# y's transposes queued behind the convolution's copies, loads a step further ahead of the sums

## The chip, the cores and the metric

The kernel runs on one core of a Trainium2 chip. The metric is the device time of one launch in microseconds. The version before took 1355.53 us (median of three runs, 1351.73 to 1358.41). Its profile was taken on one further execution of 1354.19 us, whose trace spans 1352.3 us.

## The reference, cut to what matters

```python
# x: (8, 4160, 192) f32, weight: (8, 7); w_in: (192, 1024) f64, w_out: (1024, 192) f64, g_ln: (1024,)
w = softmax(weight, axis=-1)                       # per head: 7 taps
x_pad = concatenate([zeros((B, 6, D)), x], axis=1) # causal, each of 8 batches by itself
y = einsum('hk,bskhg->bshg', w, windows of x_pad)  # 8 heads of 24 columns
h = y.reshape(33280, 192) @ w_in
e = exp(h - max(h)); solu = h * e / (sum(e) + 1e-9)
ln = (solu - mean(solu)) / sqrt(var(solu) + 1e-6) * g_ln
out = ln @ w_out                                   # (33280, 192) f32
```

## The kernel before

**Tiles, steps, chunks.** The 33280 rows are 260 tiles of 128 rows. From tile 8 on the loop takes three tiles a step (`three_steps`, tiles i, i+1, i+2, called a, b and c; i = 8, 11, 14, ...). x comes in 17 chunks: chunks 0 to 2 have 8, 8 and 16 tiles, chunks 3 to 14 have 16, the last two 18. Since 16 is no multiple of three, the steps cut the chunks in three ways that take turns. In chunks 3, 6, 9 and 12 tiles 12, 13, 14 are a step and tile 15 stands in the next one, ahead of tiles 0 and 1 of the chunk that follows (kind A). In chunks 2, 5, 8 and 11 tiles 13, 14, 15 are a step (kind B). In chunks 4, 7, 10 and 13 tiles 11, 12, 13 are one and 14, 15, 0 the next (kind C).

**What a tile passes through.** TensorE multiplies the transposed y (`yT`) with w_in in two f16 parts, `whi` and `wlo`, into `ph` (L813, L836; the smaller third part also reads `y2`). VectorE takes the row maximum (L867, `emit_max`), ScalarE the exponential (L874), VectorE the product (L884), ScalarE the f16 upper part `p` (L892) and the squares (L896), GpSimd the f16 rest (L904). SyncE then issues the DMA that transposes p into `pT` (L906). Three to five tiles later TensorE multiplies pT with w_out into `po` (L936), VectorE empties that bank (L946), GpSimd scales the rows (L1015), SyncE stores two tiles at a time (L1028).

**What a chunk passes through, ahead of its tiles.** Chunks from 3 on are `Strips`. Four loads (L354, 48 partitions and 576 KB each; numbers 0 to 3) bring x into one of two buffer sets, named `xs` and `xr` in the profile, which the chunks take in turn. Loads 0 and 1 fill the two partition halves of the first tile of the set, loads 2 and 3 those of the second. Four sums on VectorE (L375, `peak` in the table) take the absolute maximum; the sums 0 and 1 each read all partitions of the first tile, so both need loads 0 and 1, and the sums 2 and 3 need loads 2 and 3. The maxima set the scale `s`. Four convolutions on TensorE (L398, into two PSUM banks `pc`), each followed by ScalarE's copy (L278, `upper`) and VectorE's (L287, `lower`), write `y16`. SyncE's DMA transposes (L427, `turn`) carry y16 into `yT` in six pieces: two halves of block 1, and two each of blocks 0 and 2; block 1 is complete after the second convolution, blocks 0 and 2 after the fourth. One plain DMA (L435, `double`) copies a part into `y2`. In seven chunks load 0 holds the start of a batch: GpSimd then clears 16 rows of it (L363), which waits for that load's landing, and GpSimd's later work stands behind.

**What sets the order.** Every engine works through its own instructions in the order in which the code emits them; all DMAs of the main loop stand in SyncE's (SP's). `chores` (from L1071) is a table: for tile k of chunk ch it lists what is done for chunks ch+1 (convolutions, open, turns), ch+2 (loads, peaks) and ch+3 (loads). A step collects the entries of its three tiles. Loads are emitted at the step's start, ahead of its stores and of its p's transposes; peaks and `lower` ahead of `emit_max(a)`. Turns collected in a step are put in the list `moves` at its end; `move()` takes one from the list at three places: behind a's p, behind b's, and at the end. The banks `pc` and `po` are two that take turns, so a product into `po` waits for VectorE's copy out of the bank.

**The beginning.** `first_two` to `fourth_two` handle tiles 0 to 7. The unused rows between the halves of the strips are cleared once by DMAs (L451, `clear`): both tiles of `xs` and three loads of chunk 3 stand ahead of tile 6's p. Chunk 4's four loads are all emitted in the step of tiles 20 to 22, the first sum of it in the same step.

Of the kernel before, what the change touches and what calls it, by code (L numbers as in the profile page):

```python
# [19 lines left out]
def kernel(  # L20
# [309 lines left out]
    class Strips(Chunk):  # L330


        def __init__(self, ch):
            self.ch = ch
            self.b, self.t0, self.n = spans[ch]
            self.nt = self.n // P
            self.np = 4
# [10 lines left out]
        def load(self, j):  # L348

            half, late, t = self.place(j)  # L350
            self.raw[j] = t
            nt, own = self.nt, slice(64 * half, 64 * half + ROWS)
            first = self.t0 + late * nt * P // 2 + Q * ((half + late) % 2) - HALO
            nc.sync.dma_start(  # L354
                t[own],
                bass.AP(
                    tensor=x.tensor, offset=first * D,
                    ap=[[D, ROWS], [2 * Q * D, nt], [1, D]],
                ),
            )  # L360
            for w in range(nt):
                if (first + HALO + 2 * Q * w) % S == 0:
                    pool.memset(t[64 * half : 64 * half + HALO, w, :], 0.0)  # L363
# [19 lines left out]
        def product(self, h, n, a, z, bank=None):  # L383

            m = self.nt // 2
            banks = [single(f"pc_{self.ch}_{h}_{late}") for late in range(2)]
# [27 lines left out]
        def lower(self, pc, h, n, a, b):  # L414
            m = self.nt // 2
            for late in range(2):
                super().lower(pc[late], h, n, late * m, (late + 1) * m)
# [644 lines left out]
    def chores(ch, k, n):  # L1062
# [29 lines left out]
        else:  # L1092
# [179 lines left out]
    def third_two(i):  # L1272
# [31 lines left out]
        clear(0, 1)  # L1304
# [8 lines left out]
    def fourth_two(i):  # L1313
# [28 lines left out]
        early.clear()  # L1342
        emit_square(t)
# [21 lines left out]
    def three_steps(i):  # L1365
# [4 lines left out]
        work = others(ts)  # L1370
        todo = [lambda q=q: (q[0], *conv(*q)) for q in work.get("conv", [])]
# [40 lines left out]
        def lowers(n):  # L1412
            for k, pc, hg in at(n):
                k.lower(pc, *hg)
# [27 lines left out]
        if soon:  # L1442
            turns()
# [89 lines left out]
        if start:  # L1533
            for k, h in work.get("peak", []):
                sum_up(k, h, i + 2)
# [16 lines left out]
        else:  # L1552
            opens()
            if not soon:
                turns()
# [98 lines left out]
```

## Time and profile before

| | |
|---|---|
| time, median of three runs | 1355.53 us |
| the profiled execution | 1354.19 us, span 1352.3 us |
| busy: TensorE / VectorE / ScalarE / GpSimd | 1160.2 / 998.4 / 961.4 / 756.3 us |
| VectorE, sums (L375) of xr and xs | 49.6 and 49.5 us, 28 each |
| p's transposes (pT<-p, SP) | 263, median 4.7 us from issue to landing |
| y's transposes (yT<-y, SP) | 102, median 3.7 us |
| moved by DMA | 234.15 MB on one hardware queue |

A row of a timeline gives the start, the length, the engine, the line, the operation and the tiles written and read, and in brackets the engine's idle time before it and what ended that. A q behind an engine's name marks its sequencer: an SP row's length is the time in which SP waits for what the DMA needs and hands it over, not the transfer's. A row of waits names who waited, for whom, the sum in us, how often, and the longest.

### The profile page before, as it was taken

To read this page: it belongs to the slowest core of one execution; us is meant where nothing else is said; L and a number is where in the kernel's file an instruction comes from. 1 tells how busy PE (TensorE), PEld (TensorE's weight loads), DVE (VectorE), ACT (ScalarE), POOL (GpSimd) and SP (SyncE) were. 2 spreads that over 40 slices of the span, in tenths; PEclk is the share of its full clock that TensorE was granted. 3 is DMA by queue.
4 is the path that set the end of the run, shared out by engine and by line. 5 is a ranking of instruction groups with operands and counts; after the bars stand their busy time and mean duration, and the time that the engine had idled before them with its cause. 6 is when DMAs were issued, how large, how long until landed. Compare 5 with 4: busy or idle time off the path is not lost.

```text
span 1352.3 us, 24085 instructions
## 1 busy us (share of the span) xinstructions
PE 1160.2 (86%) x8854; PEld 667.0 (49%) x8854; DVE 998.4 (74%) x1736; ACT 961.4 (71%) x1613; POOL 756.3 (56%) x748
## 2 busy tenths in 40 slices
PE   5958486997989979699897979889796997999998
PEld 3635243553545545355454545445453554555556
DVE  8846285885858768586886868678685886887777
ACT  7936365784867858578685768668585785888886
POOL 3445254473664746547546655656464664666774
PEclk9979888998989989899998989899897998999999
DMA  8799889999989999999999999999999999999978
GB/s 221 129 139 170 149 143 168 174 162 180 172 151 199 177 177 180 173 169 179 192 188 170 180 185 178 156 185 191 175 175 178 174 180 167 184 195 175 197 159 174
DMA packets 736180, 235.68 MB, mean 174 GB/s; under 512 B 649230, under 2 KB 734654, under 8 KB 736062
## 3 DMA queue, kind: packets, MB, share of 16 engines
q1 hardware_dynamic: 736062, 234.15, 100.2%
q8 instruction: 69, 1.13, 0.3%
q14 instruction: 49, 0.40, 0.1%
HBM read 40.50 MB, written 25.56 MB: 49 GB/s over the span
## 4 chain that ended last, share of the span: by engine, by line
PE 26%; POOL 19%; issue 17%; DMA 16%; DVE 10%; ACT 7%; SPq 6%; POOLq 0%; DVEq 0%; ACTq 0%
POOL p L904 13%; PE po L936 12%; PE ph L813 11%; DMA xr<-in_x_dram 5%; DMA xs<-in_x_dram 5%; SPq L906 4%; DVE e L884 3%; DVE ph L867 2%; POOL raw L1015 2%; ACT e L874 2%; DMA pT<-p 2%; POOL t L1007 2%; ACT p L892 2%; DMA yT<-y 2%; ACT sq L896 2%
## 5 line engine op out<-in xcount | busy, mean ns | idle before, releaser
L904 POOL TENSOR_TENSOR p<-e,p 128x1024 f16<-128x1024 f32 x257 | 546.8, 2136 | 441.3 <-ACT p L892 416.2
L936 PE MATMUL po<-ohl,pT 128*128 128x192 f16 (+1 forms) x4264 | 565.3, 291 | 92.2 <-DVE y L287 68.7
L936 PEld LDWEIGHTS <-pT 128*128 128x128 f16 x4264 | 396.3, 100 | 268.2 <-issue 98.2
L813 PE MATMUL ph<-whi,yT 128*128 128x512 f16 x1548 | 428.4, 386 | 69.4 <-DMA yT<-y 66.7
L874 ACT ACTIVATE e<-ph,sm 128x1024 f32<-128x1024 f32 x260 | 289.6, 1114 | 259.3 <-DVE ph L867 237.2
L884 DVE SCALAR_TENSOR_TENSOR e<-ph,cv,e 128x1024 f32<-128x1024 f32 x259 | 331.6, 1280 | 73.5 <-ACT e L874 65.8
L867 DVE TENSOR_SCALAR_CACHE_REDUCE ph<-ph,cv 128x1024 f32<-128x1024 f32 x259 | 328.8, 1288 | 49.3 <-PE ph L813 25.9
L813 PEld LDWEIGHTS <-yT 128*128 128x128 f16 x2064 | 193.7, 99 | 309.3 <-DMA yT<-y 72.1
L892 ACT CAST p<-e 128x1024 f16<-128x1024 f32 x257 | 267.1, 1040 | 44.5 <-DVE e L884 35.4
L896 ACT ACTIVATE sq<-e 128x1024 f32<-128x1024 f32 x260 | 274.0, 1054 | 0.2
L813 PE MATMUL ph<-wlo,yT 128*128 128x512 f16 x516 | 154.0, 380 | 0.0
L946 DVE TENSOR_REDUCE raw<-po 128x192 f32<-128x384 f32 x247 | 136.7, 553 | 18.9 <-PE po L936 18.8
L287 DVE SCALAR_TENSOR_TENSOR y<-pc,s,y 128x384 f16<-128x384 f32 (+7 forms) x158 | 77.7, 535 | 60.3 <-ACT y L278 47.7
L278 ACT ACTIVATE y<-pc,s 128x384 f16<-128x384 f32 (+7 forms) x158 | 72.3, 518 | 64.7 <-PE pc L398 46.6
L375 DVE TENSOR_REDUCE xa<-xr 128x1 f32<-128x1536 f32 (+1 forms) x28 | 49.6, 1775 | 71.4 <-DMA xr<-in_x_dram 71.4
L1015 POOL TENSOR_SCALAR raw<-raw,t 128x192 f32<-128x192 f32 x240 | 99.0, 425 | 0.0
L375 DVE TENSOR_REDUCE xa<-xs 128x1 f32<-128x1536 f32 (+1 forms) x28 | 49.5, 1775 | 57.7 <-DMA xs<-in_x_dram 55.7
L836 PE MATMUL ph<-wlo,yT 64*128 64x512 f16 x269 | 74.1, 380 | 0.2 <-DMA yT<-y 0.2
L836 PE MATMUL ph<-wlo,y 64*128 64x512 f16 x251 | 68.7, 380 | 0.0
L363 POOL MEMSET xs<- 16x192 f32 x7 | 1.7, 248 | 100.2 <-DMA xs<-in_x_dram 89.7
L1007 POOL TENSOR_TENSOR t<-t,mhalf 128x8 f32<-128x8 f32 (+2 forms) x33 | 53.5, 1622 | 2.6
L874 ACT ACTIVATION_READ_ACCUMULATOR e<-ph,sm 128x1 f32 x260 | 50.1, 193 | 0.0
(142 smaller groups left out, 490.3 us busy)
## 6 DMA issues: line engine op xcount, KB each, us to landing
out_dram<-raw SPq DMA_DIRECT2D x127, 192.0 KB, 3.6
xs<-in_x_dram SPq DMA_DIRECT2D x24, 576.0 KB, 8.1
xr<-in_x_dram SPq DMA_DIRECT2D x24, 576.0 KB, 7.7
pT<-p SPq DMA_TRANSPOSE x263, 4.7
y<-yT SPq DMA_DIRECT2D x12, 256.0 KB, 4.0
xr<-in_x_dram SPq DMA_DIRECT2D x6, 480.0 KB, 5.9
xs<-in_x_dram SPq DMA_DIRECT2D x4, 648.0 KB, 7.9
xr<-in_x_dram SPq DMA_DIRECT2D x4, 648.0 KB, 8.3
```

The lines of the kernel that those rows point to most:

```text
L375: dve.tensor_reduce(self.part[:, col : col + 1], self.raw[j][:, a:z, :], AX.XY, ALU.max, apply_absolute_value=True,)
L813: nc.tensor.matmul(bank, lhs, w[:, r, n * 512 : (n + 1) * 512], start=start and j == 0, stop=stop and j == len(ops) - 1,)
L836: nc.tensor.matmul(banks_of(t)[n], y[q, t.off : t.off + P], wlo[q, 1, n * 512 : (n + 1) * 512], start=start, stop=not start,)
L867: dve.tensor_scalar(t.ph, t.ph, t.cv[:, 0:1], None, ALU.mult, ALU.min, accum_out=t.bias)
L874: act.activation(t.e, t.ph, AF.Exp, bias=t.bias, scale=-1.0, accum_out=grp.z[:, g : g + 1])
L884: dve.scalar_tensor_tensor(t.e, t.ph, t.cv[:, 3:4], t.e, ALU.mult, ALU.mult, accum_out=t.grp.s1[:, t.g : t.g + 1],)
L892: act.copy(t.p16[:, :, 0, :], t.halves)
L896: act.activation(junk, t.e, AF.Square, accum_out=t.grp.s2[:, t.g : t.g + 1])
L904: eng.tensor_tensor(t.p16[:, :, 1, :], t.halves, t.p16[:, :, 0, :], ALU.subtract)
L936: nc.tensor.matmul(t.po[:, 0:n], t.pT[:, a, :], w, start=j == 0, stop=j == len(ops) - 1)
L946: dve.tensor_reduce(t.grp.raw[:, t.g, :], t.po[:, 0 : 2 * D].rearrange("p (a d) -> p d a", a=2), AX.X, ALU.add,)
L1015: pool.tensor_scalar(o, o, u, 1.0, ALU.mult, ALU.mult)
```

## The change

Turns are put in the list as soon as the step's first convolution is copied, and two are issued at once, ahead of a's p; `lower` is split, with one bank's copy ahead of `emit_max(a)` and the other's behind it. The table moves loads, turns, and some peaks. Chunk 3's loads and clears at the beginning are spread over three steps. A step has at most one peak ahead of `emit_max(a)`; more go to its end. A counter with an assertion has no instruction.

```diff
             if c1:
-                fixed("open", [4], [c1])
-                fixed("turn", [q + late for q in (4, 4, 7, 9, 9, 12, 12)], [
+                fixed("open", [3 + late], [c1])
+                fixed("turn", [q + late for q in (3, 3, 6, 9, 9, 9, 9)], [
                     (c1, q) for q in (
                         (1, 0, m), (1, m, 2 * m), (3, 0, 2 * m), (0, 0, m), (2, 0, m),
                         (0, m, 2 * m), (2, m, 2 * m),
...
-                fixed("load", (4, 4, 6, 6) if late else (-1, -1, 1, 3), [(c2, j) for j in range(4)])
-                fixed("peak", (6, 7, 9, 10) if late else (1, 4, 7, 10),
+                fixed("load", (1, 2, 4, 5) if late else (-1, -1, -1, 1), [(c2, j) for j in range(4)])
+                fixed("peak", (7, 8, 10, 12) if late else (1, 4, 7, 10),
...
-                fixed("load", (13, 14), [(c3, 0), (c3, 1)])
+                fixed("load", [q + late for q in (12, 13, 15 - late)], [(c3, j) for j in range(3)])
         if ch == 0:
-            put(0.5, 0.875, "load", [(c3, j) for j in range(4)])
+            fixed("load", (6, 7), [(c3, 0), (c3, 1)])
         if ch == 1:
-            fixed("peak", (0, 1, 3, 4), [(c2, h) for j in range(4) for h in c2.halves(j)])
+            fixed("load", (0, 1), [(c2, 2), (c2, 3)])
+            fixed("peak", (3, 4, 5, 6), [(c2, h) for j in range(4) for h in c2.halves(j)])
...
         if not start:
             root_squares()
-            for k, h in work.get("peak", []):
+            opens()
+            for k, h in peaks[:1]:
                 sum_up(k, h, i + 2)
-            lowers(0)
+            lowers(0, lates=(0,))
             emit_max(a)
+            lowers(0, lates=(1,))
+            turns()
+            move()
+            move()
...
-        if start:
-            for k, h in work.get("peak", []):
-                sum_up(k, h, i + 2)
+        for k, h in peaks if start else peaks[1:]:
+            sum_up(k, h, i + 2)
```

`late` is true in chunk 2 alone. `clear(0, 1)` moves from `third_two` to the end of `fourth_two`. Three places show what this makes of SP's order.

**A chunk of kind A, tiles 41 to 46** (chunk 3, tiles 9 to 14; `yT_4` is y of the next chunk, `xr` receives chunk 6, `out` are stores). SP before:

```order
L906 DMA_TRANSPOSE pT_41_2572<-p16_41_2569 128x16x128
L1028 DMA out_0_dram<-raw_24_1871 128x2x192
L906 DMA_TRANSPOSE pT_42_2599<-p16_42_2596 128x16x128
L906 DMA_TRANSPOSE pT_43_2639<-p16_43_2636 128x16x128
L427 DMA_TRANSPOSE yT_4_2317<-y16_73 128x8x128
L354 DMA xr_72<-in_x_dram 48x16x192 x2
L1028 DMA out_0_dram<-raw_24_1871 128x2x192
L906 DMA_TRANSPOSE pT_44_2710<-p16_44_2707 128x16x128
L427 DMA_TRANSPOSE yT_4_2317<-y16_73 128x8x128
L1028 DMA out_0_dram<-raw_32_2309 128x2x192
L906 DMA_TRANSPOSE pT_45_2745<-p16_45_2742 128x16x128
L906 DMA_TRANSPOSE pT_46_2786<-p16_46_2783 128x16x128
```

And SP now, from two turns ahead of the same tile 41:

```order
L429 DMA_TRANSPOSE yT_4_2233<-y16_73 128x8x128 x2
L908 DMA_TRANSPOSE pT_41_2574<-p16_41_2571 128x16x128
L429 DMA_TRANSPOSE yT_4_2233<-y16_73 128x8x128
L1030 DMA out_0_dram<-raw_24_1875 128x2x192
L908 DMA_TRANSPOSE pT_42_2602<-p16_42_2599 128x16x128
L429 DMA_TRANSPOSE yT_4_2233<-y16_73 128x8x128
L908 DMA_TRANSPOSE pT_43_2643<-p16_43_2640 128x16x128
L355 DMA xr_72<-in_x_dram 48x16x192 x2
L1030 DMA out_0_dram<-raw_24_1875 128x2x192
L908 DMA_TRANSPOSE pT_44_2713<-p16_44_2710 128x16x128
L1030 DMA out_0_dram<-raw_32_2313 128x2x192
L908 DMA_TRANSPOSE pT_45_2747<-p16_45_2744 128x16x128
```

All four turns of blocks 0 and 2 now stand among the p's of tiles 41 to 43; loads 0 and 1 stay behind tile 43's p. Behind tile 46's p, where one load stood, two stand now (loads 2 and 3).

**A chunk of kind C, tiles 58 to 62** (chunk 4, tiles 10 to 14; `xs` receives chunk 7). SP before:

```order
L906 DMA_TRANSPOSE pT_58_3430<-p16_58_3427 128x16x128
L427 DMA_TRANSPOSE yT_5_3107<-y16_73 128x8x128
L354 DMA xs_0_419<-in_x_dram 48x16x192
L1028 DMA out_0_dram<-raw_40_2731 128x2x192
L906 DMA_TRANSPOSE pT_59_3499<-p16_59_3496 128x16x128
L427 DMA_TRANSPOSE yT_5_3107<-y16_73 128x8x128
L906 DMA_TRANSPOSE pT_60_3532<-p16_60_3529 128x16x128
L906 DMA_TRANSPOSE pT_61_3571<-p16_61_3568 128x16x128
L427 DMA_TRANSPOSE yT_5_3107<-y16_73 128x8x128
L354 DMA xs_0_419<-in_x_dram 48x16x192
L906 DMA_TRANSPOSE pT_62_3661<-p16_62_3658 128x16x128
```

And SP now:

```order
L908 DMA_TRANSPOSE pT_58_3434<-p16_58_3431 128x16x128
L355 DMA xs_0_419<-in_x_dram 48x16x192 x2
L1030 DMA out_0_dram<-raw_40_2733 128x2x192
L908 DMA_TRANSPOSE pT_59_3503<-p16_59_3500 128x16x128
L908 DMA_TRANSPOSE pT_60_3535<-p16_60_3532 128x16x128
L908 DMA_TRANSPOSE pT_61_3574<-p16_61_3571 128x16x128
L355 DMA xs_1_420<-in_x_dram 48x16x192
L908 DMA_TRANSPOSE pT_62_3663<-p16_62_3660 128x16x128
```

Load 1 moves a whole step ahead, beside load 0; load 2 takes its old place, and the turns are gone from here. In kind B (not shown) load 0 goes a step ahead, and load 1 leads load 2 where loads 0 and 1 stood.

**The first chunks, tiles 17 to 20** (`xr<-zero` are clears, `xr` receives chunk 4). SP before:

```order
L451 DMA xr_72<-zero_91 16x18x192 x2
L1028 DMA out_0_dram<-raw_0_538 128x2x192
L906 DMA_TRANSPOSE pT_17_1296<-p16_17_1293 128x16x128
L1028 DMA out_0_dram<-raw_0_538 128x2x192
L906 DMA_TRANSPOSE pT_18_1323<-p16_18_1320 128x16x128
L328 DMA y2_2_968<-yT_2_967 64x896
L906 DMA_TRANSPOSE pT_19_1364<-p16_19_1361 128x16x128
L354 DMA xr_72<-in_x_dram 48x16x192 x4
L1028 DMA out_0_dram<-raw_0_538 128x2x192
L906 DMA_TRANSPOSE pT_20_1458<-p16_20_1455 128x16x128
```

And SP now:

```order
L453 DMA xr_72<-zero_91 16x18x192 x2
L355 DMA xr_72<-in_x_dram 48x16x192 x2
L1030 DMA out_0_dram<-raw_0_538 128x2x192
L908 DMA_TRANSPOSE pT_17_1298<-p16_17_1295 128x16x128
L1030 DMA out_0_dram<-raw_0_538 128x2x192
L908 DMA_TRANSPOSE pT_18_1325<-p16_18_1322 128x16x128
L328 DMA y2_2_965<-yT_2_964 64x896
L908 DMA_TRANSPOSE pT_19_1366<-p16_19_1363 128x16x128
L355 DMA xr_72<-in_x_dram 48x16x192 x2
L1030 DMA out_0_dram<-raw_0_538 128x2x192
L429 DMA_TRANSPOSE yT_3_1440<-y16_73 128x8x128 x2
L908 DMA_TRANSPOSE pT_20_1460<-p16_20_1457 128x16x128
```

Two of the four loads go a step ahead, behind the clears, and the first sum that needs them stands a step later than before (tile 7 of chunk 2 in place of tile 6).

More of the change, by code (lines that the diff above doesn't have):

```diff
@@ L336, in __init__ @@
             self.nt = self.n // P
-            self.np = 4
+            self.np, self.convs = 4, 0
             self.raw = [None] * self.np
@@ L351, in load @@
             self.raw[j] = t
+            assert self.ch < OLD + 2 or chunks[self.ch - 2].convs == 4
             nt, own = self.nt, slice(64 * half, 64 * half + ROWS)
@@ L385, in product @@
             m = self.nt // 2
+            self.convs += 1
             banks = [single(f"pc_{self.ch}_{h}_{late}") for late in range(2)]
@@ L412, in upper, with lower @@
                 super().upper(pc[late], h, n, late * m, (late + 1) * m)
-        def lower(self, pc, h, n, a, b):
+        def lower(self, pc, h, n, a, b, lates=(0, 1)):
             m = self.nt // 2
-            for late in range(2):
+            for late in lates:
                 super().lower(pc[late], h, n, late * m, (late + 1) * m)
@@ L1303, in third_two @@
         clear(0, 0)
-        clear(0, 1)
         for q in (t, u):
@@ L1342, in fourth_two @@
         early.clear()
+        clear(0, 1)
         emit_square(t)
@@ L1370, in three_steps @@
         work = others(ts)
+        peaks = work.get("peak", [])
         todo = [lambda q=q: (q[0], *conv(*q)) for q in work.get("conv", [])]
@@ L1410, in uppers, with lowers @@
                 k.upper(pc, *hg)
-        def lowers(n):
+        def lowers(n, **which):
             for k, pc, hg in at(n):
-                k.lower(pc, *hg)
+                k.lower(pc, *hg, **which)
         def move():
@@ L1440, in openings @@
                 move()
-        if soon:
-            turns()
         run_stores()
@@ L1552, in three_steps @@
         else:
-            opens()
-            if not soon:
-                turns()
             move()
```

## The prediction

> **What bounds the kernel now.** First the page's head and its chain of waits by engine:
>
> ```profile
> span 1352.3 us, 24085 instructions
> PE 1160.2 (86%) x8854; PEld 667.0 (49%) x8854; DVE 998.4 (74%) x1736; ACT 961.4 (71%) x1613; POOL 756.3 (56%) x748
> PE 26%; POOL 19%; issue 17%; DMA 16%; DVE 10%; ACT 7%; SPq 6%; POOLq 0%; DVEq 0%; ACTq 0%
> ```
>
> TensorE is the busiest, yet the chain runs 16% of the span through DMAs. The view of waits says which:
>
> ```profile
> POOL xs L363 <- DMA xs<-in_x_dram: 89.7, 6, 23.6
> DVE xa L375 <- DMA xr<-in_x_dram: 71.4, 11, 17.3
> PE po L936 <- DVE y L287: 68.7, 14, 16.3
> PE ph L813 <- DMA yT<-y: 66.7, 11, 12.3
> DVE xa L375 <- DMA xs<-in_x_dram: 55.7, 10, 10.6
> PE po L936 <- DMA pT<-p: 19.8, 5, 16.9
> ```
>
> VectorE's sums wait 71.4 + 55.7 = 127.1 us for loads. TensorE waits 66.7 us for y's transposes, and 68.7 us for a bank that VectorE frees in `lower`, which stands behind the waiting sum. These lie partly at the same time, so they can't be added. I take whole stretches instead, in the view of windows, for the exponentials alone (stretch, its length, their busy time, x counts two instructions a tile, TensorE's granted clock, DMA share, GB/s):
>
> ```profile
> 536.30:577.20 40.90, 7.23 (x12) 0.87 1.09 179
> 459.60:484.70 25.10, 3.62 (x6) 0.85 1.13 175
> 385.80:410.30 24.50, 3.62 (x6) 0.83 0.98 168
> 1132.60:1197.40 64.80, 18.07 (x30) 0.98 1.11 184
> 1247.20:1318.70 71.50, 21.69 (x36) 1.00 0.95 180
> ```
>
> The fourth has convolutions and sums but no loads any more: 30/2 = 15 tiles, five steps, 64.80/5 = 13.0 us a step. The fifth has neither: 71.50/6 = 11.9. The first is the end of a chunk of kind A: two steps take 40.9 us, 15.0 more than 2 x 13.0. The second is B: one step, 25.1, 12.1 lost. The third is C: 24.5, 11.5 lost. So each chunk loses about one step's time once, where it ends. Twelve chunks (2 to 13, four of a kind) load during their tiles, so about 4 x (15.0 + 12.1 + 11.5) = 154 us lie there.
>
> **Kind A, price 3.5 us of the 15.0.** SP's timeline at the end of chunk 3, then VectorE's and TensorE's rows there:
>
> ```profile
> 285.70 0.87 SPq L435 DMA_DIRECT2D y<-yT  x1
> ...
> 291.72 6.68 SPq L906 DMA_TRANSPOSE pT<-p  x2
> 298.45 1.30 SPq L427 DMA_TRANSPOSE yT<-y  x1
> 299.80 1.18 SPq L354 DMA_DIRECT2D xr<-in_x_dram  x2
> 301.69 9.31 SPq L906 DMA_TRANSPOSE pT<-p  x1
> 311.10 1.25 SPq L427 DMA_TRANSPOSE yT<-y  x1
> ...
> 311.32 1.75 DVE L375 TENSOR_REDUCE xa<-xr 128x1 f32<-128x1536 f32 x1 [8.79 <-DMA xr<-in_x_dram]
> ...
> 314.26 1.89 PE L813 MATMUL ph<-whi,yT 128*128 128x512 f16 x4 [8.77 <-DMA yT<-y]
> ```
>
> Two loads are handed over at 299.80. The next p's transpose is stuck on SP until 311.0, y's turn behind it goes at 311.10, and TensorE waits for that turn until 314.26. VectorE meanwhile waits for the second load until 311.32. Two waits of 8.8 us stand side by side, and after them TensorE still has its late products to do: this makes 15.0 of them. The change takes the turn away from behind the loads, so TensorE's 8.77 go. VectorE's 8.79 stay: loads 0 and 1 are still in the step just ahead of the first sum. They are not handed over earlier either: the turn directly ahead (1.30) goes, but three more turns than before (1.3 each) and no `double` (0.87, the first row) stand among the three p's ahead, 3 x 1.3 - 0.9 - 1.3 = some 2 us later. So 8.8 + 2, and 1 more for the second pair one step on (below), are kept: 11.5 of 15.0, a gain of 3.5. Bounds: nothing, or a loss of 3 if the second pair holds p's for more; at best 9, if SP has the turns done in its idle time and the wait shrinks to 6.
>
> **Kind B, 6.5 us of 12.1.** The chain of waits shows a second load of a pair from hand-over to landing, in chunk 5 and chunk 8, and the tile view gives the landing of all xr loads:
>
> ```profile
> 469.88 10.35 DMA xr<-in_x_dram
> 707.32 11.37 DMA xs<-in_x_dram
> DMA to landing us min/median/max: 1.9/7.3/17.1
> ```
>
> Now load 0 is a step earlier and load 1 leads load 2, so the sum needs the first of a pair: 7.3 in place of 10.4 to 11.4, some 3.5 us sooner; the turn ahead (1.3) is gone, and so are the turns behind. The gain is 3.5 + 1.3 + about 1.7 of TensorE's restart = 6.5. Bounds: 2 (if the load leading is slowed by the one behind) and 11. Chunk 2 is of kind B but issues three loads together, with loads 0 and 1 first: like A it keeps the sum's wait, but TensorE's longest wait for yT, the 12.3 of the waits above, is there, and I take 6 for it (0 to 12).
>
> **Kind C, 6.5 us of 11.5.** Loads 0 and 1 are now two steps, some 25 us, ahead of the sum, more than twice a pair's landing: the sum's wait goes, and the turns too. What is late next is p: the 9.31 us row shows that a pair of loads holds a p's transpose on SP. A tile is multiplied with w_out about one step after its p is handed over, 11.9 us, and p lands in 4.7:
>
> ```profile
> pT<-p SPq DMA_TRANSPOSE x263, 4.7
> ```
>
> That leaves 11.9 - 4.7 = 7.2 us of cover, so a pair costs TensorE 9.3 - 7.2 = 2 us, and the two single loads in the next steps some 3 by the same queue. Kept: 5, gained 6.5. Bounds: a loss of 3 (no cover at all) and 10.
>
> **The four loads of chunk 4, 10 us.** SP hands over the clears and the four loads in these rows:
>
> ```profile
> 142.62 1.28 SPq L451 DMA_DIRECT2D xr<-zero  x2
> ...
> 158.75 4.72 SPq L354 DMA_DIRECT2D xr<-in_x_dram  x4
> ```
>
> The first sum stands in the same step and waits 17.3 us, the longest of its kind. Now two loads go a step ahead, the sum a step behind, and the wait goes. In its place the pair behind the clears holds the p of tile 17 (in the same stretch TensorE waits 16.3 for a bank, the longest of that row: also gone). I charge a pair's 9.3 less 2 for the step's slack: 17.3 - 7.3 = 10. Bounds 0 and 17.
>
> **The beginning, nothing.** Rows of SP:
>
> ```profile
> 62.95 6.26 SPq L451 DMA_DIRECT2D xs<-zero  x4
> 69.26 5.79 SPq L354 DMA_DIRECT2D xs<-in_x_dram  x3
> 82.69 4.76 SPq L906 DMA_TRANSPOSE pT<-p  x1
> ```
>
> Tile 6's p waits here for GpSimd, which waits 23.6 us for a landing, and TensorE 16.9 for that p. Now p of tiles 6 and 7 goes ahead. But the same clears and loads then stand ahead of tiles 8 and 9, and three of chunk 3's four sums are collected behind them in the step of tiles 11 to 13. I expect the wait to move from tile 6 to tile 9: 0, with bounds of a gain of 15 and a loss of 5.
>
> **The rest** costs nothing: the same instructions run on each engine, `lower` for the second bank is done while TensorE is busy with b's product, and the maximum of a comes one such copy earlier. The two turns ahead of a's p wait for that copy, which ends several VectorE operations before a's p is ready; if VectorE is held by a sum there, p is held with it.
>
> **Sum.** 4 x 3.5 + (3 x 6.5 + 6) + 4 x 6.5 + 10 + 0 = 75.5 us. Against the profiled execution: 1354.2 - 75.5 = 1278.7. The median is 1.3 above that execution, so I say 1280.
>
> **Rivals.** *The queue turns against it (slower).* A p behind loads waits for them. If it has no cover, each pair costs its full 9.3 us, each single load about 4 (the longest landing above, 17.1, is that of the last of four handed over together), in place of what is lost now: A with two pairs 18.6 for 15.0, B with a pair and two singles 17.3 for 12.1, C the same for 11.5. That is 4 x (3.6 + 5.2 + 5.8) = 58 us, less the 10 of chunk 4's loads and the 4 x 3.5 of A's turns: 1388. It decides from the point at which p's cover falls below about 2 us. Against it: TensorE waited for pT only 5 times before, 19.8 us, 16.9 of them at the beginning, although pairs held p then as well. For it: now there are two pairs in a row in A. The Trainium skill speaks for this one: its page "DMA: Bandwidth & Descriptors", section "Queues, rings and completion order", says that the issuing engine has one ring on each DMA engine and that descriptors are consumed in ring order; by that rule alone, without cover, it would be 1388, and the row of 9.31 us agrees that a transpose waits behind loads, but not that TensorE does.
>
> *Only the turns help.* If the sums of B and C still wait as A's do, each chunk gains 3.5: 12 x 3.5 + 5 = 47, 1307. For it: the windows show a DMA share near 1 everywhere, so an earlier load may take longer. Against it: C's loads have two steps.
>
> *DMA is the limit, no change.* The lost stretches move 168 to 179 GB/s, the one without loads 184. Were 179 the most that these small pieces allow, the waits would only move: 1354. Against it: 184 and 180 were reached while TensorE had no gaps, and the lost stretches' TensorE clock was 0.83 to 0.87, against 0.98 to 1.00 where it ran through, which speaks of idle time, not of a full machine everywhere.
>
> *More than I count.* A's wait shrinks to 6, B's goes, the beginning gains 10: 1235.
>
> **How the numbers follow.** Forecast 0.58, only the turns 0.21, full DMA 0.07, the queue against it 0.08, more than counted 0.06. The range that leaves out most of the slower rival and half of the best case is 1235 to 1330. About 0.5% is what a measurement of this kernel can tell from no change. Faster by over that: 0.85; within it 0.07; slower 0.08.
>
> **What would show it.** In the profile after, TensorE's wait for yT should fall from 66.7 to under 10 us. VectorE's wait for xr and xs should fall from 127 to about 60, and what is left should stand at the first sum of A and B and be gone in C. TensorE's wait for pT should rise from 19.8 to 30 to 60. A wait for pT above 100 would show the slower rival; waits for loads in C, the second. The forecast is wrong if the windows at the chunks' ends still show a step of 24 us.

## The result and the profile after

| | before | after |
|---|---|---|
| median | 1356.22 us (1351.73 to 1358.41, 4 runs) | 1301.11 us (1299.32 to 1302.67, 4 runs) |
| profiled execution | 1354.19 us | 1300.94 us |

The ratio is 0.9597, 95% interval 0.957 to 0.9625: 55 us faster, where 75 were forecast. Head and chain of the changed kernel's page:

```profile
span 1299.2 us, 24145 instructions
PE 1154.4 (89%) x8854; PEld 665.9 (51%) x8854; DVE 994.1 (77%) x1736; ACT 954.8 (73%) x1613; POOL 756.3 (58%) x748
PE 42%; DMA 17%; POOL 15%; issue 12%; DVE 7%; ACT 4%; SPq 3%; DVEq 0%; POOLq 0%; ACTq 0%
```

TensorE does the same work in a shorter span and carries 42% of the chain in place of 26. The DMAs' share has not fallen (16% to 17%): the waits have moved, as the view of waits shows.

```profile
POOL xs L364 <- DMA xs<-in_x_dram: 92.1, 6, 25.9
...
PE po L938 <- DMA pT<-p: 67.7, 32, 10.1
...
PE po L938 <- DVE y L287: 49.7, 9, 8.9
...
DVE xa L376 <- DMA xr<-in_x_dram: 29.0, 4, 9.7
...
DVE xa L376 <- DMA xs<-in_x_dram: 21.7, 3, 10.0
```

The page's group of the first products (busy us, mean ns, then idle time before) no longer has a wait for yT, where 66.7 us stood:

```profile
L815 PE MATMUL ph<-whi,yT 128*128 128x512 f16 x1548 | 421.4, 381 | 3.8 <-DVE e L886 2.6
```

The sums' wait for loads fell from 127.1 to 50.7. The wait for p's transposes rose from 19.8 (5 times) to 67.7 (32 times). The same windows as before, for the exponentials (length, busy, clock, DMA share, GB/s): the chunk ends of kind A, B and C that the prediction showed, the step of tiles 194 to 196, and the stretch without convolutions.

```profile
505.50:541.10 35.60, 7.23 (x12) 0.90 1.05 172
435.10:454.90 19.80, 3.61 (x6) 1.00 1.20 164
366.20:386.00 19.80, 3.61 (x6) 0.83 1.08 178
1002.20:1021.10 18.90, 3.61 (x6) 0.82 1.23 189
1205.90:1277.40 71.50, 21.70 (x36) 1.00 0.89 161
```

The three ends went from 40.9, 25.1 and 24.5 to 35.6, 19.8 and 19.8. The fourth row is a step that took 13.4 before: something is given back. The last one is as before, to the tenth.

I did this for every step (the time from the first exponential of a step to that of the next, in both traces) and added it up by place. For A it is the two steps of each end, for B one, for C three, so that a wait that moves to the next step is caught:

| place | before | after | difference | forecast |
|---|---|---|---|---|
| A, four ends | 163.4 | 145.2 | -18.2 | -14 |
| B, three ends | 72.5 | 62.4 | -10.1 | -19.5 |
| chunk 2's end | 41.6 | 36.1 | -5.5 | -6 |
| C, four ends | 204.0 | 179.6 | -24.4 | -26 |
| chunk 4's loads (tiles 17 to 28) | 68.6 | 61.1 | -7.5 | -10 |
| beginning (to tile 16) | 144.4 | 146.2 | +1.8 | 0 |
| all other steps (the last one, with the program's end, left out) | 636.2 | 647.2 | +11.0 | 0 |

What a kind-A end looks like now, in chunk 3, where the prediction read SP, VectorE and TensorE; SP first, then the sum, then TensorE:

```profile
285.20 2.71 SPq L908 DMA_TRANSPOSE pT<-p  x1
287.94 1.32 SPq L355 DMA_DIRECT2D xr<-in_x_dram  x2
289.32 0.52 SPq L1030 DMA_DIRECT2D out_dram<-raw  x1
289.96 8.83 SPq L908 DMA_TRANSPOSE pT<-p  x1
...
299.03 1.75 DVE L376 TENSOR_REDUCE xa<-xr 128x1 f32<-128x1536 f32 x1 [9.28 <-DMA xr<-in_x_dram]
...
301.36 3.72 PE L938 MATMUL po<-ohl,pT 128*128 128x384 f16 x16 [7.46 <-DVE y L287]
```

No turn stands behind the pair any more, and TensorE has its yT. But the sum still waits 9.28 us for the pair, and as `lower` stands behind it, TensorE waits 7.46 for the bank. The 8.83 us of p's row on SP are not all the pair's: the waits of SP in this stretch (289.9 to 299) put 3.1 of them down to GpSimd, which hadn't finished that p.

```profile
SPq L908 <- POOL raw L1017: 3.1, 1, 3.1
```

### The profile page after: what moved, and what is told of

Its sections match the earlier page's. It is cut to its first block, busy times and chain, and to the rows that moved or that the text cites. A ratio compares the mean times of both kernels' runs of the same rounds, so it can differ in the third digit from the quotient of the medians.

```text
span 1299.2 us, 24145 instructions
## 1 busy us (share of the span) xinstructions
PE 1154.4 (89%) x8854; PEld 665.9 (51%) x8854; DVE 994.1 (77%) x1736; ACT 954.8 (73%) x1613; POOL 756.3 (58%) x748
## 4 chain that ended last, share of the span: by engine, by line
PE 42%; DMA 17%; POOL 15%; issue 12%; DVE 7%; ACT 4%; SPq 3%; DVEq 0%; POOLq 0%; ACTq 0%
PE po L938 20%; PE ph L815 17%; POOL p L906 10%; DMA pT<-p 9%; DMA xs<-in_x_dram 4%; DVE ph L869 3%; DMA xr<-in_x_dram 3%; PE ph L838 2%; SPq L908 2%; PE pc L400 2%; POOL raw L1017 2%; ACT p L894 2%; POOL t L1009 2%; DVE y L287 1%; DVE e L886 1%
## 5 line engine op out<-in xcount | busy, mean ns | idle before, releaser
L938 PE MATMUL po<-ohl,pT 128*128 128x192 f16 (+1 forms) x4264 | 573.2, 293 | 119.5 <-DMA pT<-p 67.7
L815 PE MATMUL ph<-whi,yT 128*128 128x512 f16 x1548 | 421.4, 381 | 3.8 <-DVE e L886 2.6
L886 DVE SCALAR_TENSOR_TENSOR e<-ph,cv,e 128x1024 f32<-128x1024 f32 x259 | 331.4, 1280 | 61.7 <-ACT e L876 61.0
L869 DVE TENSOR_SCALAR_CACHE_REDUCE ph<-ph,cv 128x1024 f32<-128x1024 f32 x259 | 332.8, 1287 | 35.6 <-PE ph L838 27.6
L287 DVE SCALAR_TENSOR_TENSOR y<-pc,s,y 128x384 f16<-128x384 f32 (+7 forms) x158 | 82.0, 537 | 55.1 <-ACT y L278 54.7
L364 POOL MEMSET xs<- 16x192 f32 x7 | 1.7, 247 | 103.7 <-DMA xs<-in_x_dram 92.1
```

What stands on the lines that cost most here:

```text
L815: nc.tensor.matmul(bank, lhs, w[:, r, n * 512 : (n + 1) * 512], start=start and j == 0, stop=stop and j == len(ops) - 1,)
L869: dve.tensor_scalar(t.ph, t.ph, t.cv[:, 0:1], None, ALU.mult, ALU.min, accum_out=t.bias)
L886: dve.scalar_tensor_tensor(t.e, t.ph, t.cv[:, 3:4], t.e, ALU.mult, ALU.mult, accum_out=t.grp.s1[:, t.g : t.g + 1],)
L938: nc.tensor.matmul(t.po[:, 0:n], t.pT[:, a, :], w, start=j == 0, stop=j == len(ops) - 1)
```

## The experiments

For the first group my theory was that each part pays for the waits that it takes away, 38 us for the turns and 36 for the loads. The rivals were that the turns carry nearly all and an earlier load only changes the place of a wait, or that the parts need each other. For the later groups the question is what a load costs: its place beside other loads, its bytes, SP's line or the DMA engines. The kernel before ran beside each group: medians 1353.62, 1353.21, 1354.28 and 1352.68 us.

### Each half of the change alone

The turns alone: the table's loads and peaks, the peaks' place and the beginning as before. The earlier `open` and the split `lower` stay with the turns; they were not tried apart.

```diff
-                fixed("load", (1, 2, 4, 5) if late else (-1, -1, -1, 1), [(c2, j) for j in range(4)])
-                fixed("peak", (7, 8, 10, 12) if late else (1, 4, 7, 10),
+                fixed("load", (4, 4, 6, 6) if late else (-1, -1, 1, 3), [(c2, j) for j in range(4)])
+                fixed("peak", (6, 7, 9, 10) if late else (1, 4, 7, 10),
...
-                fixed("load", [q + late for q in (12, 13, 15 - late)], [(c3, j) for j in range(3)])
+                fixed("load", (13, 14), [(c3, 0), (c3, 1)])
```

> The turns' part alone (turns and open in the table, the two moves ahead of a's p, the split copies); loads, sums and the beginning as before. Theory (each part pays for the waits that it takes away): TensorE's 66.7 us of waits for yT go, VectorE's 127 for loads stay. About 5 us go in each chunk of kind A and in chunk 2, 2 to 3 in B and C: 38 us, 1318 us. Rival (the turns carry nearly all, earlier loads only change the place of a wait): 1301 to 1308. Rival (the sums hold everything anyway, the turns alone are worth nothing): 1350 or more.

Measured: 1311.22 us, ratio 0.9686 [0.9651, 0.9721], between the theory (1318) and the rival in which the turns carry nearly all (1301 to 1308). Its waits:

```profile
PE po L938 <- DVE y L287: 90.8, 18, 16.7
...
DVE xa L376 <- DMA xr<-in_x_dram: 62.3, 11, 17.6
DVE xa L376 <- DMA xs<-in_x_dram: 48.8, 10, 9.0
...
PE po L938 <- DMA pT<-p: 35.4, 15, 15.8
```

The sums wait nearly as long as before (111.1 for 127.1), and yet 42 of the 55 us are there. By the same count of steps: A -13.4, B -14.9, C -19.0, other steps +13.5. So most of C's gain needs no earlier load, and in B the turns alone gain more than the whole change (-10.1).

The loads alone: the entries for `open` and `turn` and the places of `turns()`, `move()` and `lower` as before.

```diff
-                fixed("open", [3 + late], [c1])
-                fixed("turn", [q + late for q in (3, 3, 6, 9, 9, 9, 9)], [
+                fixed("open", [4], [c1])
+                fixed("turn", [q + late for q in (4, 4, 7, 9, 9, 12, 12)], [
```

> Loads, sums and the beginning as changed, turns and copies as before. Theory: the sums' waits fall to about 50 us as in the changed kernel, TensorE's for yT stay near 50 and more: 8 us of chunk 4's loads, 4 in each B and C chunk, nothing in A: 36 us, 1320 us. Rival (earlier loads only move a wait): 1345 or more. If the two parts help each other, both this and the turns alone lie above 1325.

Measured: 1359.0 us, ratio 1.0035 [1.0015, 1.0054]: not the theory (1320) but the rival, an earlier load that only moves a wait (1345 or more).

```profile
PE ph L815 <- DMA yT<-y: 79.1, 11, 15.1
...
DVE xa L376 <- DMA xr<-in_x_dram: 33.3, 4, 9.0
DVE xa L376 <- DMA xs<-in_x_dram: 31.7, 4, 8.6
```

The sums' waits are halved, and nothing is gained: TensorE's wait for yT rises from 66.7 to 79.1. By the count of steps, chunk 4's loads gain 11.7 us and the other steps 12.9, and the chunks' ends lose it again: A +15.5, B +3.6, C +9.1. In A two pairs of loads in a row now have a turn behind them, where it was one pair and a single load. Between the two alone, 1311.2 for the turns and 1301.1 for both, the loads are worth 10 us, and only with the turns out of their way.

### The first sum a step later

```diff
-                fixed("peak", (7, 8, 10, 12) if late else (1, 4, 7, 10),
+                fixed("peak", (7, 8, 10, 12) if late else (4, 7, 10, 11),
```

> The changed kernel with the four sums of a chunk at tiles 4, 7, 10, 11 in place of 1, 4, 7, 10, so that in kinds A and B the first sum stands a step further behind its loads. Theory (in A and B the step that is still long is long for the wait of the first sum, 9.4 us in A, 3 to 5 in B): the sums' wait falls from 50.7 to under 10 us and 40 to 46 us go, less some 8 that p's transposes then wait more: 1262 to 1270. Rival (p's transposes behind the pairs of loads are as late as the sum): the wait goes to pT, 1290 to 1301.

Measured: 1298.66 us, ratio 0.9596 [0.957, 0.9622], the changed kernel's own. The theory (1262 to 1270) missed; the rival (the wait goes to pT, 1290 to 1301) came true. The sums' waits for loads are gone from the rows; the time stands here instead:

```profile
PEld L938 <- DMA pT<-p: 129.1, 50, 10.1
DVE raw L948 <- PE po L938: 115.8, 60, 8.3
PE po L938 <- DMA pT<-p: 106.3, 41, 9.7
```

TensorE's wait for pT rises by 38.6 us (67.7 to 106.3), its weight loads' from 85.0 to 129.1. What costs is the pair, not the place of the sum.

### GpSimd's clearing at the step's end

```diff
-                    pool.memset(t[64 * half : 64 * half + HALO, w, :], 0.0)
+                    wipes.append(
+                        lambda w=w: pool.memset(t[64 * half : 64 * half + HALO, w, :], 0.0)
+                    )
...
         emit_lo(c, pool)
+        while wipes:
+            wipes.pop(0)()
```

> The changed kernel with GpSimd's clearing of 16 rows (where a batch starts) emitted at the end of the step, behind c's p, in place of directly behind the load. Theory (GpSimd's wait of 92 us is mostly parallel with SP being held by the same loads, only chunk 8 and 10 show it, 23.9 and 19.7 us against 19 and 16.5): GpSimd's wait falls below 20, 8 to 12 us go, about 1291. Rival (wholly covered): 1301. Rival (it is on the path each of the six times): 1270 or less.

Measured: 1286.16 us, ratio 0.9507 [0.9481, 0.9533]: 15 us below the changed kernel, where I had expected 8 to 12. What the clearing did there is seen in the changed kernel's timelines, in chunk 10 (SP, GpSimd, SP, TensorE):

```profile
817.58 1.14 SPq L355 DMA_DIRECT2D xs<-in_x_dram  x2
...
824.82 0.25 POOL L364 MEMSET xs<- 16x192 f32 x1 [12.38 <-DMA xs<-in_x_dram]
825.04 2.12 POOL L906 TENSOR_TENSOR p<-e,p 128x1024 f16<-128x1024 f32 x1
...
827.18 4.88 SPq L908 DMA_TRANSPOSE pT<-p  x2
...
831.50 4.82 PE L938 MATMUL po<-ohl,pT 128*128 128x384 f16 x19 [3.79 <-DMA pT<-p]
```

A clearing of 0.25 us starts at 824.82, when its load has landed. Behind it stands the lower half of p, whose transpose SP can hand over only from 827.18 on, ten us after the loads, and TensorE waits 3.79 for that pT. With the clearing at the step's end its wait for loads falls from 92.1 to 18.0:

```profile
POOL xs L367 <- DMA xs<-in_x_dram: 18.0, 6, 8.6
```

### One load in a step

```diff
-                fixed("load", (1, 2, 4, 5) if late else (-1, -1, -1, 1), [(c2, j) for j in range(4)])
-                fixed("peak", (7, 8, 10, 12) if late else (1, 4, 7, 10),
+                fixed("load", (1, 2, 4, 5) if late else (-1, -1, 2, 5), [(c2, j) for j in range(4)])
+                fixed("peak", (7, 8, 10, 12) if late else (5, 8, 11, 13),
...
-                fixed("load", [q + late for q in (12, 13, 15 - late)], [(c3, j) for j in range(3)])
+                fixed("load", (12 + late, 15), [(c3, 0), (c3, 1)])
```

> Edit: the changed kernel with one strip load in a step instead of two or three: the second chunk ahead's loads 2 and 3 move to steps 2 and 5 of the chunk, the third chunk ahead's to steps 12 and 15, and every maximum to two steps or more behind its load. The number and the bytes of the loads stay. Theory 'bunches' (the loss left is that two loads in one step hold SP's queue for about 11 us, so that a sum, or the transpose of p behind them, comes late, while one load alone holds it 4 to 5 us and hides): both the sums' waits for xr and xs (29.0 and 21.7 us in the changed kernel) and PE's waits for pT (67.7 us) fall below a third, each of the ten chunks goes from some 76.7 us to 70 to 72, and the time is 1240 to 1265 us. Rival 'bytes' (each load costs its transfer's time wherever it stands, because p's transposes share the queue with it): the waits for the sums go, those for pT rise by as much, and the time stays within 1290 to 1310. Rival 'too early': the sum's buffers or GpSimd's clearing then waits for the convolution that reads them, and the time rises above 1310.

Measured: 1298.01 us, ratio 0.9595 [0.9572, 0.9618]. My expectation "bunches" (1240 to 1265) missed, and the rival "bytes" (1290 to 1310) came true: the sums no longer wait, but pT is waited for 62 times:

```profile
PE po L938 <- DMA pT<-p: 105.0, 62, 8.1
```

The same with the late clearing:

> Edit: the spread of the loads, one in a step, together with GpSimd's clearing of the strips' first rows given out at the end of the step. Clearing late alone gave 1286.2 us, 15 below the changed kernel. If the two losses are different ones (GpSimd stands behind the load; SP's queue is full of loads), the gains add: 1225 to 1250. If they are the same loss seen twice (p's lower half late because GpSimd or the queue behind it is late), this stands within 5 us of the better of the two alone. If 'bytes' holds, 1275 to 1292.

Measured: 1270.45 us, ratio 0.9376 [0.9348, 0.9404], which is none of my three (1225 to 1250 if the gains add, 1275 to 1292 by "bytes", or the better of the two alone). It is 27.6 below the spread alone and 15.7 below the late clearing alone. So the spread is worth something once GpSimd doesn't wait for the load: the gains alone, 3.1 and 15.0 us, do more than add. What is left is a wait for pT of 1.4 us at a time, 65 times:

```profile
PE po L942 <- DMA pT<-p: 93.4, 65, 10.1
```

### The loads behind the first p

`loads(work)` stands behind a's p instead of at the step's start:

```diff
-        if not start:
-            loads(work)
         got = {}
...
-        if start:
-            loads(work)
-        else:
+        loads(work)
+        if not start:
             second()
             uppers(2)
```

> Edit: the changed kernel with the step's loads issued behind the transpose of the step's first p instead of at the step's start; turns, sums and counts are the same. If a pair of loads costs because the p of the first tile stands behind it in SP's queue, its pT comes in time: PE's waits for pT fall from 67.7 us to below 40 and the time to 1285 to 1295. If the queue's time counts wherever it is spent, the second and third p of the step and the sums come later instead: the waits for xr and xs rise above 70 us together and the time is 1300 to 1320.

Measured: 1346.03 us, ratio 0.9936 [0.9904, 0.9968]. Both expectations missed; the second has the direction, not the size.

```profile
PE po L938 <- DMA pT<-p: 77.7, 22, 9.2
PE po L938 <- DVE y L287: 71.9, 9, 12.3
...
DVE xa L376 <- DMA xs<-in_x_dram: 44.0, 4, 13.5
DVE xa L376 <- DMA xr<-in_x_dram: 38.5, 4, 12.4
```

The waits for loads rise from 50.7 to 82.5, and the wait for pT rises as well (67.7 to 77.7): the loads come later in the step, and b's and c's p now stand directly behind them. Nearly the whole gain of the change hangs on this place.

### Without loads, with half of each, in two halves, by another engine

These take the cost of the loads itself apart. First the changed kernel without the loads of ten chunks:

```diff
         def load(self, j):
 
             half, late, t = self.place(j)
             self.raw[j] = t
+            if 5 <= self.ch < 15:
+                return
```

> Edit: the changed kernel without the strip loads, and the clearing that goes with them, of chunks 5 to 14; the maxima and the convolutions of these chunks work on rows that stand there from earlier. It measures what all the loads of ten chunks still cost. The chunks without loads (0 and the last ones) run at some 69 us for 16 tiles against 76.7 us in the changed kernel: both theories expect 1215 to 1240. If the time comes out above 1280 the loads are nearly free already and what is left at the chunks' ends is the turns' own; if it comes out below 1210 the loads also cost in steps that show no wait for them.

Measured: 1203.49 us, ratio 0.8892 [0.8874, 0.891], 12 us below the 1215 to 1240 that I expected; a time below 1210, I had written, would mean that loads also cost in steps that show no wait for them. Then two edits of the kernel with spread loads and late clearing (1270.45): half of the rows of each load of the same ten chunks, and each of these loads as two halves, the second behind b's p.

```diff
+            part = nt if not 5 <= self.ch < 15 else nt // 2
             nc.sync.dma_start(
-                t[own],
+                t[own, 0:part],
...
-                    ap=[[D, ROWS], [2 * Q * D, nt], [1, D]],
+                    ap=[[D, ROWS], [2 * Q * D, part], [1, D]],
```

> Edit: the kernel with one load in a step and the late clearing (1270.5 us), in which the loads of chunks 5 to 14 bring only the first half of their rows (288 KB instead of 576), so that the other half of the sums and of the convolution works on rows that stand there from earlier. As many loads, half their packets. If the cost goes by packets or bytes ('engines', or 'queue' with the hold as long as the load): half of the 67 us between 1270.5 and 1203.5 us goes, 1232 to 1245. If it goes by the number of loads (a fixed hold of each): 1260 to 1272. If the engines are full only above a limit, the first half of the load is free and nearly all goes: 1200 to 1215.

Measured: 1214.02 us, ratio 0.8962 [0.894, 0.8983]. This is the range of the third theory, that the first half of a load is nearly free (1200 to 1215). Half of the bytes takes away 56 of the 67 us between 1270.45 and 1203.49. (1203.49 is the changed kernel without its loads; the one with spread loads was not run without them, so the 67 us are a measure with that reserve.)

In the second edit `rows(a, z)` loads the rows from a to z:

```diff
...
+            if 5 <= self.ch < 15:
+                rows(0, nt // 2)
+                seconds.append(lambda: rows(nt // 2, nt))
+            else:
+                rows(0, nt)
...
         emit_lo(b, pool)
+        while seconds:
+            seconds.pop(0)()
         move()
```

> Edit: the kernel with one load in a step and the late clearing (1270.5 us), in which each load of chunks 5 to 14 is two loads of 288 KB in the same step, the first at its start as before, the second behind the transpose of the second p. The bytes stay; each piece is as long as those of the half loads (4.8 us to landing), which cost next to nothing (1214.0 us). Theory 'hold' (a whole load holds p longer than the 7.2 us that hide it, a half one does not): the halves hide too, 1214 to 1240, PE's waits for pT below 50 us. Theory 'engines full' (in the steady chunks the DMA engines move 191 to 193 GB/s with the loads and with half of them alike, so what they bring above that is paid by its bytes wherever it stands): 1262 to 1280, waits for pT 80 to 105 us. In between, both take part.

Measured: 1242.9 us, ratio 0.919 [0.9162, 0.9217], with the whole output computed: the fastest version of this study, 58 below the changed kernel, and between the two theories (to 1240 and from 1262). The windows from 300 to 700 us of, in this order, the changed kernel, the one without loads, whole loads spread, half of them, and two halves (busy time and instructions of TensorE first; the last three numbers are clock, DMA share and GB/s):

```profile
300.00:700.00 400.00, 367.86 (x2885) 208.65 (x2885) 317.25 (x538) 300.17 (x504) 242.20 (x239) 0.96 1.09 187
```
```profile
300.00:700.00 400.00, 399.55 (x3259) 230.24 (x3258) 353.63 (x602) 338.41 (x568) 273.90 (x269) 1.00 0.96 177
```
```profile
300.00:700.00 400.00, 371.01 (x2946) 204.97 (x2944) 323.60 (x544) 305.44 (x511) 246.65 (x243) 1.00 1.11 192
```
```profile
300.00:700.00 400.00, 397.55 (x3198) 226.66 (x3196) 349.57 (x592) 331.72 (x555) 269.30 (x265) 1.00 1.05 192
```
```profile
300.00:700.00 400.00, 384.44 (x3054) 217.10 (x3053) 337.04 (x565) 318.60 (x533) 258.36 (x253) 0.99 1.10 200
```

Without loads (and the clearing that goes with them) TensorE has next to no gaps (399.55 of 400). With half of them it has few (397.55), at 192 GB/s. Whole loads move the same 192 GB/s while TensorE has 29 us of gaps; so 192 is no limit of the engines here, and indeed the two halves bring 200. Cutting a load in two, with the same bytes, gains 27.6 of the 56.4 us that half of the bytes gains, and TensorE waits for pT less often:

```profile
PE po L949 <- DMA pT<-p: 70.4, 42, 8.6
```

So about half of what the second half of each load costs goes when it comes as a piece of its own, behind b's p; the rest stays with the bytes in this order of work. The cut and the later place were not told apart (whole loads behind a's p, in the changed kernel, lost 45 us), and a finer cut was not tried.

Is the hold SP's line, or the DMA engines? The loads are issued by ScalarE, in the spread version and in the changed kernel:

```diff
-            nc.sync.dma_start(
+            nc.scalar.dma_start(
                 t[own],
```

> Edit: the kernel with one load in a step and the late clearing (1270.5 us), the strip loads issued by ScalarE instead of SyncE; number, size and place in the step as there. Theory 'queue' (a load costs because p's transposes stand behind it in SyncE's own line; without the loads the time was 1203.5): transposes no longer stand behind loads, PE's waits for pT fall from 93 us to below 50 and the time to 1215 to 1245. Theory 'engines' (the 16 DMA engines themselves are full: their share is 105.8% with the loads and 96.6% without): the loads take the same packets' time from the same engines, the waits for pT stay at 80 to 110 us and the time within 1262 to 1280. Rival: ScalarE's issuing or its own line delays the copies behind it, the time rises above 1280.

> Edit: the changed kernel (1301.1 us), its strip loads issued by ScalarE instead of SyncE, in the same steps and in the same bunches of two or three. Theory 'queue': the p behind a pair is no longer held, the sums' waits stay as the pair itself lands no earlier: 1265 to 1285. Theory 'engines': 1295 to 1310, with the sums' waits for xr and xs together near 50 us as before and pT's near 68.

Measured: 1300.72 us, ratio 0.9599 [0.9558, 0.9639], against 1270.45; and 1323.24, ratio 0.9777 [0.9748, 0.9807], against 1301.11. To see the hold itself I took each transpose of p between 300 and 1000 us whose landing the trace records, from the moment SP had all that it waits for, by the trace's releasers (or began the row, if later), to the landing, in two groups: a load under way that lands at least 2 us later, or no such load. The medians, with the counts:

| kernel | no such load | a load under way |
|---|---|---|
| whole loads spread, on SP | 4.3 us (120) | 6.3 us (10) |
| the same, issued by ScalarE | 4.4 us (106) | 6.5 us (22) |
| two halves, on SP | 3.9 us (116) | 5.5 us (15) |

A load delays a p by some 2 us, and by as much when SP never issued it. So SP's line does not make this hold, and "queue" falls: the hold lies in what both lines share. The spread version's wait for pT stays where "engines" put it (80 to 110):

```profile
PE po L942 <- DMA pT<-p: 82.7, 47, 8.2
```

What the lines share is told by the Trainium skill on its page "DMA: Bandwidth & Descriptors", section "Queues, rings and completion order": the SP and ACT queues each have a ring on the same 16 engines, not engines of their own. The trace agrees with it in the 6.5 us beside 6.3; where on this way the time goes it does not show.

But both times came out above what "engines" expected, 1300.72 by 21 us (over 1280, the range of the rival that ScalarE's own line is delayed) and 1323.24 by 13 (over 1310). In the changed kernel with ScalarE's loads the waits are not those that "engines" named either: the sums' waits for loads (about 50 expected) are gone, and TensorE's for pT (68 expected) is the longest of all versions. A row stands there that the changed kernel lacked, ScalarE's squares waiting:

```profile
PE po L938 <- DMA pT<-p: 120.3, 39, 12.5
...
ACT sq L898 <- DMA pT<-p: 44.6, 8, 9.8
```

The squares do not read pT. All eight waits stand directly behind the second load of a pair, which ScalarE handed over only when a p had landed, as in chunk 3:

```profile
274.71 10.75 ACTq L355 DMA_DIRECT2D xr<-in_x_dram  x2
285.51 1.06 ACT L898 ACTIVATE sq<-e 128x1024 f32<-128x1024 f32 x1 [9.76 <-DMA pT<-p]
```

So here the rival is at work: ScalarE's own line is stopped by a load that it issues. How much of the 22.1 us above the changed kernel this makes was not measured. In the spread version, with one load in a step, no such row of squares and pT stands, and its 30.3 us stay open.

## Why the prediction was right, and where not

The direction and the mechanism of A hold, and 1301.1 lies in the range 1235 to 1330. The size holds less well: 55 us of 75, and the sum hides terms that were wrong both ways.

- **A, 3.5 each.** Right, a little low: 4.6 each (3.4 with the turns alone). TensorE's wait for yT went, VectorE's 8.79 stayed, as 9.28.
- **B, 6.5 each.** Mis-sized: 3.4 each. The step that failed is "the sum needs the first of a pair ... some 3.5 us sooner". The turns alone gained 5.0 in B, not the 1.3 + 1.7 that I gave them (for the 1.7 of TensorE's restart no run shows a row): the first sum's wait fell from 9.1 to 11.4 us to 4.7 to 7.3 with the loads where they were. The earlier loads took only some 1.5 us more from it (3.3 to 5.0), and they brought waits for pT of 2.1 and 5.2 us in chunks 5 and 8, which the turns alone don't have. The longer one stands behind the clearing in chunk 8 (below): that step takes 23.9 us, with the late clearing 19.5, and with it B's three ends gain 15.1, 5.0 each.
- **C, 6.5 each.** The size is right (6.1), the reason only partly. The turns alone gained 4.8 with the sums still waiting 3.9 to 5.9 us. The loads' two steps added 1.4: the sum's wait is gone, and one for pT of 3.3 to 4.1 us stands there instead.
- **Chunk 4's loads, 10.** 7.5; TensorE's wait for pT of 7.0 us, in the step of tiles 23 to 25, is the charge that I had set at 9.3 less 2.
- **The beginning, 0.** Right, +1.8, and the wait moved as said.
- **The rest, 0.** Wrong, and the largest miss beside B: 11 us were given back in steps that hardly waited before. With the turns alone it is 13.5 us, and with the loads alone these steps are 12.9 shorter, so the loads' new places are not the cause. With the late clearing 4.8 us are left of the 11.0, and the step of tiles 194 to 196 is back at 13.2. Without loads these steps take 627.7 in place of 647.2. So the turns beside the p's, the loads and the clearing make it together. In the steps of tiles 116 and 164 TensorE waits twice for pT, 1.1 to 1.3 us each; my argument looked at VectorE's copy, not at what else the DMA engines carry there.
- **The signs.** TensorE's wait for yT below 10 us: yes. The sums' waits at about 60: 50.7, and all seven at the first sum of A and B, none in C. pT's at 30 to 60: 67.7, a little above. No step of 24 us at the chunks' ends: not quite. A's first steps are still 21.9 to 23.5, as their sum waits, and one of B's, chunk 8's, is 23.9.

Of the rivals, "only the turns help" (1307) lies nearer to 1301.1 than the forecast does, and the turns alone gave 1311.2; its condition fails, though, as the sums of C no longer wait and those of B less than half as long. "The queue turns against it" was not the outcome, but transposes are late behind loads, as it says, in two runs: y's with the loads alone (79.1 us), p's with the later sum (106.3). Its price for a p behind a pair, 9.31 us, was read wrongly. The waits of SP in that row's stretch (301.5 to 312, kernel before) show GpSimd in it:

```profile
SPq L906 <- POOL raw L1015: 4.2, 1, 4.2
```

Only 5.1 of the 9.31 can be the pair's. The cover of 7.2 us was wrong the other way: by it a delay of 2 us would cost nothing, and with whole loads spread TensorE waits 65 times (whether for the delay alone or for a p that is itself late was not taken apart). The two errors nearly cancel in the 5 us kept in C; that C's size came out is partly luck.

The clearing, which costs 15 us here and 27.6 with the loads spread, appeared in the prediction's first quoted row of waits (89.7 us), and I put no price on it. Its waits are nearly as long after (92.1), but not all at the same place. In chunk 8 load 0 goes a step ahead and takes the clearing along, ahead of the lower halves of p of that step's own tiles (changed kernel; SP, GpSimd, SP, TensorE):

```profile
657.13 0.90 SPq L355 DMA_DIRECT2D xs<-in_x_dram  x1
...
664.10 0.25 POOL L364 MEMSET xs<- 16x192 f32 x1 [11.63 <-PE po L938]
...
666.46 7.12 SPq L908 DMA_TRANSPOSE pT<-p  x3
...
670.98 3.38 PE L938 MATMUL po<-ohl,pT 128*128 128x384 f16 x13 [5.20 <-DMA pT<-p]
```

The load landed at 663.99; the row names TensorE, whose semaphore changed last (664.07). Three p's are handed over only after it, and TensorE waits 5.2 us. Of all that I left out, the clearing was the cheapest thing to mend.

## What to carry to other kernels

When a transfer is late, look at everything that is handed over beside it: moving small transposes out from behind big loads gave 42 us, moving the loads earlier without that gave nothing. A wait that vanishes at one reader is worth only what does not turn up at the next (a sum's 50.7 us became 38.6 more for pT). If short transfers that TensorE needs soon share the DMA engines with long ones, cut the long ones into pieces between them (27.6 us here), and let no engine that produces the short ones wait for the long ones' landing (15.0 us).

## What was not expected of the hardware

- Loads issued by another engine delayed SP's transposes all the same (6.5 us to landing, 6.3 with all on SP), and the kernel was slower by 30.3 and 22.1 us than with all of them on SP. In the second of these ScalarE's line stood for up to 9.8 us behind a load that it issues.
- Half of the bytes of the loads cost 10.5 us (1214.02 against 1203.49 without loads), the other half 56.4. With half loads the DMA engines moved 192 GB/s while TensorE was busy 397.55 of 400 us; the same GB/s in whole loads left gaps of 29 us.
- The DMA share in the windows stands above 1 whether TensorE has gaps or not (from 300 to 700 us 1.09 in the changed kernel, 1.10 in the version with two halves, 1.05 with half of each load): here neither it nor the GB/s (192 with gaps and without) tells whether the engines limit; only TensorE's gaps show whether the loads cost time.
